# Key softmax of batches 1 to 3 with keys on partitions, short matmul bursts at fixed places, and the second product three pairs behind the first

## The chip, the cores and the metric

The kernel runs on one core of one Trainium2 chip. The metric is the device time in microseconds of one execution. All times here are in us unless marked ns.

## The reference

Four batches of agent attention (12480 queries and keys of 128 channels, 49 agents) feed a two-layer network with an odd nonlinearity.

```python
def attn(q, k, v, agents):                 # B=4, N=12480, C=128, 49 agents
    sm = lambda a, b: softmax((a @ b.transpose(0, 2, 1)) / sqrt(128))
    return sm(q, agents) @ (sm(agents, k) @ v)
def moe(x, w_in, w_out):                   # 49920 tokens, 128 -> 2048 -> 128
    h = x @ w_in
    return (h - tanh(h)) @ w_out
out = moe(attn(q, k, v, agents).reshape(-1, 128), w_in, w_out)
```

All inputs and the output are float32.

## The kernel before

**The main stream.** The 49920 tokens are cut into 100 blocks of 500 (the last block of a batch has 480). The small matrix `agent_v @ w_in` of a batch is formed once (`project`) and split into a rounded part `awh` and a remainder `awl`, so that two fast matmuls (type fp32r) do the work of an exact one. A block then takes 8 *pairs* of 128 hidden channels. One pair is:

- `m1` on TensorE: four matmuls of 500 columns into `h` (PSUM, three buffers), lines 538 and 539;
- `y` (tanh) and `z` (square) on ScalarE, lines 548 and 550; `g = h * z` on VectorE, line 553;
- `gh`, the rounded copy of `g`, on GpSimd, line 582; `gl = g - gh` on VectorE, line 587;
- `m2` on TensorE: six matmuls of 500 columns (lines 600 to 602) that add into the block's accumulator, a `misc` tile in PSUM (two buffers, shared with every short-lived product below).

One pair of every second block (the plain pair) skips the split and uses float32 matmuls at line 598. Two blocks, 16 pairs, make one period of everything else; there are 50 periods.

**Work beside the stream.** In each period, 1000 queries go through a softmax over the agents (`q_softmax`: a burst of 32 small float32 products on TensorE, line 494, which show as 64 matmuls in the trace; then `qm`, `qe`, `qs` and `pp` on VectorE, ScalarE and GpSimd, lines 502 to 517), and are transposed (`q_transpose`, line 525). While batch b runs through the stream, the key softmax of batch b+1 is done in between (`phase1`), in jobs that `fast` starts at three places of a period (`KS` for the scores, `VS` for the rest). A batch has 98 tiles of 128 keys, in 13 groups of 8 tiles (the last of 2).

**The key softmax of batches 1 to 3 before.** The scores of a group lie with *agents* on partitions: `agz` (49 agents padded to 64 columns) is stationary and the keys move past it (line 279); two tiles fill the 128 partitions, 512 columns a group. ScalarE copies them to `s` (281), VectorE takes a maximum (282). After all groups one maximum over everything is formed on VectorE (290 to 295). Then, a group at a time, `av`: ScalarE's exp (324), four transposes on TensorE (330) to bring the keys to partitions, a copy out of PSUM on ScalarE (333), the product with `v` on TensorE (340, whose stationary operand is the transposed e), and an addition into `acc` on VectorE (352).

**Order.** The program is written as generators; each `yield` ends a step, and each pair of the main loop advances every live job by one step. A planner that simulates the engines then sets the order of each engine's queue; `hold` ties an instruction behind another one. Each engine then runs its queue strictly in that order. `LAG1` and `LAG2` say how many pairs `gl` and `m2` are written behind; `NB` gives the numbers of buffers.

Of the kernel before, what the change touches and what calls it, by code (L numbers as in the profile page):

```python
# [12 lines left out]
F32 = mybir.dt.float32  # L13
# [47 lines left out]
LAG2 = 1  # L61
NB = dict(y=2, z=2, g=4, gh=3, gl=2)
# [4 lines left out]
QS = 3  # L67
T0 = 13
T1 = 2
KS = (4, 10, 15)  # L70
VS = (5, 10, 13)
# [26 lines left out]
class Build:  # L98
    def __init__(self, ctx, tc, aps):
# [7 lines left out]
        self.pmisc = ctx.enter_context(self.pool("pmisc", 2, space=PSUM))  # L107

# [9 lines left out]
    def constants(self):  # L118
        nc = self.nc
        c = self.const  # L120
        self.agz = c.tile([128, B, HALF], F32, tag="ag", name="ag")
        self.ag = self.agz[:, :, :A]
        nc.sync.dma_start(self.ag, self.agT.rearrange("b c a -> c b a"))
        nc.gpsimd.memset(self.agz[:, :, A:], 0.0)
# [71 lines left out]
    def phase1(self, b):  # L196
# [36 lines left out]
        def scores(g):  # L233
            yield
            yield
            if g == 0:
                st["s"] = self.keep.tile([128, NG * 512], F32, tag="s", name="s", bufs=1)
                if b == 0:
                    st["mxp"] = self.work.tile([128, A, 2 * NG], F32, tag="mxp", name="mxp", bufs=1)
                else:  # L240
                    st["mxp"] = self.small.tile([128, NG], F32, tag="mxk", name="mxk")
                st["acc"] = self.small.tile([128, C + 1], F32, tag="acc", name="acc")
# [32 lines left out]
            w = n // 2 * 128  # L275
            for c in range(n // 2):
                for r in range(2):
                    to = ps[HALF * r : HALF * (r + 1), c * 128 : (c + 1) * 128]
                    nc.tensor.matmul(to, self.agz[:, b, :], kt[:, n // 2 * r + c, :], start=True, stop=True)  # L279
            yield  # L280
            nc.scalar.copy(st["s"][:, g * 512 : g * 512 + w], ps[:, :w])
            nc.vector.tensor_reduce(st["mxp"][:, g : g + 1], ps[:, :w], axis=AX.X, op=ALU.max)

        def max_in():
            yield
            yield
            if b:
                m = self.small.tile([128, 1], F32, tag="mk", name="mk")
                top = self.small.tile([128, 1], F32, tag="mt", name="mt")
                nc.vector.tensor_reduce(m, st["mxp"], axis=AX.X, op=ALU.max)  # L290
                nc.vector.tensor_copy(top[:HALF], m[HALF:])
                nc.vector.tensor_tensor(m[:HALF], m[:HALF], top[:HALF], ALU.max)
                nc.vector.tensor_copy(m[HALF:], m[:HALF])
                st["mb"] = self.small.tile([128, 1], F32, tag="mn", name="mn")
                nc.vector.tensor_scalar(st["mb"], m, -SCALE, None, ALU.mult)
                return
            m = self.small.tile([128, A], F32, tag="m", name="m")
            nc.vector.tensor_reduce(m, st["mxp"][:, :, 2 * EARLY :], axis=AX.X, op=ALU.max)
# [18 lines left out]
        def av(g):  # L317
            vt = ahead("v", load_v, g, vb - 1) if b else None
            n = tiles(g)
            if b:  # L320
                w = n // 2 * 128
                e = st["s"][:, g * 512 : g * 512 + w]
                first = self.count()
                nc.scalar.activation(e, e, AF.Exp, bias=st["mb"], scale=SCALE)
                self.hold(first, self.act_at, (ET.Activation,))
                yield
                ps = self.misc()
                for c in range(n // 2):
                    sl = slice(c * 128, (c + 1) * 128)
                    nc.tensor.transpose(ps[:, sl], e[:, sl], self.ident)  # L330
                yield
                et = self.small.tile([128, 512], F32, tag="ke", name="ke")
                nc.scalar.copy(et[:, :w], ps[:, :w])
                yield
                ps = self.misc()
                for c in range(n // 2):
                    for r in range(2):
                        t = n // 2 * r + c
                        k = rows(g, t)
                        nc.tensor.matmul(  # L340
                            ps[HALF * r : HALF * (r + 1), : C + 1],
                            et[:k, c * 128 + HALF * r : c * 128 + HALF * (r + 1)],
                            vt[:k, t, : C + 1],
                            start=c == 0,
                            stop=c == n // 2 - 1,
                        )
                yield
                acc = st["acc"]
                if g == 0:
                    nc.vector.tensor_copy(acc, ps[:, : C + 1])  # L350
                else:
                    nc.vector.tensor_tensor(acc, acc, ps[:, : C + 1], ALU.add)
                return
            sv = st["s"][:, g * GT * A : (g * GT + n) * A].rearrange("p (t a) -> p t a", a=A)
            e3 = sv
            nc.vector.tensor_tensor(e3, sv, st["mb"][:, None, :].broadcast_to([128, n, A]), ALU.subtract)
            yield
            nc.scalar.activation(e3, e3, AF.Exp, scale=SCALE)
            yield
# [5 lines left out]
            flat = e3.rearrange("p t a -> p (t a)")  # L365
# [19 lines left out]
            if g in (2, 3):  # L385
                st["es", g % 2] = self.small.tile([128, GT * A], F32, tag="ke", name="es")
# [11 lines left out]
        def sums():  # L398
# [19 lines left out]
            acc = st["acc"]  # L418
# [488 lines left out]
```

## Time and profile before

| | us |
|---|---|
| three runs | 2139.34, 2142.42, 2142.45; median 2142.42 |
| profiled execution | 2142.99, span of the engines' work 2141.2 |
| TensorE matmuls busy | 2107.2 (98%) |
| VectorE busy | 1996.0 (93%) |
| ScalarE busy | 1820.5 (85%) |
| GpSimd busy | 1303.9 (61%) |

The stream's first matmul starts 55.5 us after the span's start; batch 0's key softmax fills the time before it. Matmul ends are modelled, so the busy time of TensorE says only that it is seldom without work; how fast it goes is read from start to start in the timeline. On the other engines a busy time is the engine's own. A wait is put down to the instruction that ended it.

### The profile page before, as it was taken

The page shows a single profiled execution, that of the slowest core. Times are in us where ns is not written, and L with a number is a line of the kernel's source. Part 1 is how long each engine was busy: PE and PEld are TensorE (multiplying, and loading weights), DVE is VectorE, ACT ScalarE, POOL GpSimd, SP SyncE. Part 2 cuts the span into 40 slices and gives each one's busy share as a digit, 9 for nine tenths or more (in the row PEclk, how much of TensorE's full clock was granted, in tenths as well). Part 3 has the DMA queues.
Part 4 walks back from the last instruction along what each step waited for, and adds up shares of the span by engine and source line. Part 5 has one row for each costly group of instructions (what it writes and reads, how often), then busy time and mean ns, then how long its engine had stood idle before and what let it go on. Part 6 is the DMA issues. An engine that isn't in the chain of part 4 may idle for free.

```text
span 2141.2 us, 35133 instructions
## 1 busy us (share of the span) xinstructions
PE 2107.2 (98%) x13259; PEld 1658.2 (77%) x13259; DVE 1996.0 (93%) x2031; ACT 1820.5 (85%) x2136; POOL 1303.9 (61%) x858
## 2 busy tenths in 40 slices
PE   8999999999999999999999999999999999999998
PEld 7577778777777777777787777777777777778776
DVE  7899999889999998889999999988999999999998
ACT  3888888888888888888898888888888989899897
POOL 0366666556665556556576566655666767767666
PEclk9999999999999999999999999999999999999999
DMA  9312112110112111211001110111000000100000
GB/s 343 105 60 68 53 37 72 51 55 24 39 49 67 54 50 50 59 61 49 20 28 61 59 42 30 50 59 42 30 30 21 29 30 20 33 26 20 30 10 21
DMA packets 65345, 109.01 MB, mean 51 GB/s; under 512 B 3984, under 2 KB 44176, under 8 KB 65168
## 3 DMA queue, kind: packets, MB, share of 16 engines
q1 hardware_dynamic: 65168, 106.68, 15.2%
q8 instruction: 108, 1.77, 0.4%
q14 instruction: 69, 0.57, 0.1%
HBM read 81.10 MB, written 25.56 MB: 50 GB/s over the span
## 4 chain that ended last, share of the span: by engine, by line
PE 66%; DVE 18%; issue 6%; POOL 5%; ACT 4%; DMA 0%; POOLq 0%; SPq 0%; DVEq 0%; ACTq 0%
PE misc L602 12%; PE h L538 11%; PE misc L600 11%; PE h L539 11%; PE misc L601 10%; DVE g L553 9%; DVE gl L587 6%; POOL gh L582 4%; PE misc L598 3%; ACT y L548 2%; PE misc L340 2%; PE misc L494 2%; ACT z L550 1%; PE misc L279 1%; PE h L250 1%
## 5 line engine op out<-in xcount | busy, mean ns | idle before, releaser
L582 POOL TENSOR_SCALAR gh<-g 128x1000 fp32r<-128x1000 f32 (+1 forms) x743 | 1197.8, 1612 | 690.2 <-DVE g L553 387.5
L587 DVE TENSOR_TENSOR gl<-g,gh 128x1000 fp32r<-128x1000 f32 (+1 forms) x743 | 956.5, 1287 | 85.6 <-PE misc L602 42.9
L553 DVE TENSOR_TENSOR g<-h,z 128x1000 f32<-128x1000 f32 (+1 forms) x800 | 945.4, 1188 | 30.8 <-ACT z L550 28.8
L548 ACT ACTIVATE y<-h 128x1000 f32<-128x1000 f32 (+1 forms) x800 | 801.4, 1004 | 198.4 <-PE h L539 192.0
L550 ACT ACTIVATE z<-y 128x1000 f32<-128x1000 f32 (+1 forms) x800 | 823.1, 1041 | 29.2 <-DVE g L553 12.9
L538 PE MATMUL h<-pT,awh 98*128 98x500 f32 (+1 forms) x1600 | 662.5, 414 | 0.3
L539 PE MATMUL h<-pT,awl 98*128 98x500 f32 (+1 forms) x1600 | 622.0, 389 | 0.0
L602 PE MATMUL misc<-gl,wo_h 128*128 128x500 f32 (+1 forms) x1486 | 594.4, 400 | 8.2 <-DVE gl L587 7.9
L600 PE MATMUL misc<-gh,wo_l 128*128 128x500 f32 (+1 forms) x1486 | 581.7, 391 | 7.6 <-POOL gh L582 6.7
L601 PE MATMUL misc<-gh,wo_h 128*128 128x500 f32 (+1 forms) x1486 | 578.2, 389 | 0.0
L538 PEld LDWEIGHTS h<-pT,awh 98*128 98x128 f32 x1600 | 301.2, 188 | 79.8 <-issue 17.7
L539 PEld LDWEIGHTS h<-pT,awl 98*128 98x128 f32 x1600 | 303.3, 190 | 68.9 <-issue 14.5
L602 PEld LDWEIGHTS misc<-gl,wo_h 128*128 128x128 f32 x1486 | 279.0, 188 | 83.3 <-DVE gl L587 23.1
L600 PEld LDWEIGHTS misc<-gh,wo_l 128*128 128x128 f32 x1486 | 280.6, 189 | 75.3 <-POOL gh L582 21.6
L601 PEld LDWEIGHTS misc<-gh,wo_h 128*128 128x128 f32 x1486 | 279.7, 188 | 53.6
L505 POOL TENSOR_TENSOR qe<-qe,qm 126x392 f32<-126x392 f32 x50 | 46.9, 938 | 77.2 <-ACT qe L503 77.2
L517 POOL TENSOR_TENSOR pp<-qe,pp 126x392 fp32r<-126x392 f32 x50 | 55.6, 1113 | 59.6 <-ACT pp L515 59.5
L598 PE MATMUL misc<-g,wo_f 128*128 128x500 f32 (+1 forms) x196 | 90.0, 581 | 0.0
L758 ACT ACTIVATE o<-misc 128x500 f32<-128x500 f32 (+1 forms) x100 | 58.0, 580 | 16.2 <-PE misc L602 9.0
L530 ACT CAST pT<-misc 98x500 fp32r<-98x500 f32 (+1 forms) x100 | 56.7, 568 | 5.3 <-PE misc L525 4.4
L598 PEld LDWEIGHTS misc<-g,wo_f 128*128 128x128 f32 x196 | 36.9, 188 | 26.2 <-issue 22.5
L525 PEld LDWEIGHTS misc<-identr,pp 126*98 126x98 f32 x400 | 38.9, 127 | 18.4 <-POOL pp L517 6.5
(111 smaller groups left out, 853.7 us busy)
## 6 DMA issues: line engine op xcount, KB each, us to landing
kt<-kT SPq DMA_DIRECT2D x48, 512.0 KB, 3.7
qt<-qT SPq DMA_DIRECT2D x46, 500.0 KB, 3.5
outT<-o SPq DMA_DIRECT2D x46, 500.0 KB, 2.6
v<-v SPq DMA_DIRECT2D x36, 512.0 KB, 4.1
vt<-v SPq DMA_DIRECT2D x12, 512.0 KB, 5.8
raw<-w_in SPq DMA_DIRECT2D x4, 512.0 KB, 9.2
v<-w_out SPq DMA_DIRECT2D x4, 512.0 KB, 8.1
qt<-qT SPq DMA_DIRECT2D x4, 490.0 KB, 3.5
```

Source lines behind the costliest of these rows:

```text
L538: nc.tensor.matmul(h[:, c, :w], aw[0][:A2, sl], pT[:A2, :w], start=True, stop=False)
L539: nc.tensor.matmul(h[:, c, :w], aw[1][:A2, sl], pT[:A2, :w], start=False, stop=True)
L548: nc.scalar.activation(self.pair(y), h, AF.Tanh, scale=TSC)
L550: nc.scalar.activation(z, y, AF.Square)
L553: nc.vector.tensor_tensor(self.pair(g), h, self.pair(z), ALU.mult)
L582: self.nc.gpsimd.tensor_scalar(gh, g, 1.0, 0.0, ALU.mult, ALU.add)
L587: self.nc.vector.tensor_tensor(gl, g, gh.bitcast(F32), ALU.subtract)
L598: nc.tensor.matmul(acc[:, :w], wf[:, c * C : (c + 1) * C], gh[:, x], start=first, stop=last)
L600: nc.tensor.matmul(acc[:, :w], self.wo_l[:, f, :], gh[:, x], start=first, stop=False)
L601: nc.tensor.matmul(acc[:, :w], self.wo_h[:, f, :], gh[:, x], start=False, stop=False)
L602: nc.tensor.matmul(acc[:, :w], self.wo_h[:, f, :], gl[:, x], start=False, stop=last)
L758: nc.scalar.activation(o[:, at : at + w], acc[n][:, :w], AF.Copy, scale=GSC)
```

## The change

Scores of batches 1 to 3 are now computed with *keys* on partitions: each quarter (32 keys) of a tile of keys is stationary and the 49 agents move, the same shape as the query softmax's burst. A group is 128 partitions by 392 columns in `s`. The maximum is now one for each agent: VectorE reduces each group, and `max_in` and `max_out` (a transpose and a product with a diagonal on TensorE, until now for batch 0 alone) make `mb`. `av` subtracts `mb` on GpSimd, exponentiates on ScalarE three steps later, and two steps after that uses e directly as the stationary operand of the product with `v`; the transposes and the copy behind them are gone.

`burst` chains the small matmuls of the scores, of the product with `v` and of the query scores to one another and behind the last two stream groups written, and `streamed` ties the next six stream groups behind them. `LAG2` goes from 1 to 2, `gh` from 3 to 4 buffers and `gl` from 2 to 3. `QS`, `T1`, `KS` and `VS` are other places; `q_softmax` has one step more ahead of its burst and one less behind it. The tile `s` becomes smaller.

```diff
-LAG2 = 1
-NB = dict(y=2, z=2, g=4, gh=3, gl=2)
+LAG2 = 2
+NB = dict(y=2, z=2, g=4, gh=4, gl=3)
-QS = 3
+QS = 5
-T1 = 2
-KS = (4, 10, 15)
-VS = (5, 10, 13)
+T1 = 3
+KS = (6, 9, 14)
+VS = (2, 5, 9)
...
@@ scores
-            w = n // 2 * 128
-            for c in range(n // 2):
-                for r in range(2):
-                    to = ps[HALF * r : HALF * (r + 1), c * 128 : (c + 1) * 128]
-                    nc.tensor.matmul(to, self.agz[:, b, :], kt[:, n // 2 * r + c, :], start=True, stop=True)
-            yield
-            nc.scalar.copy(st["s"][:, g * 512 : g * 512 + w], ps[:, :w])
-            nc.vector.tensor_reduce(st["mxp"][:, g : g + 1], ps[:, :w], axis=AX.X, op=ALU.max)
+            first = self.count()
+            for t in range(n):
+                for r in range(0, 128, QUART):
+                    to = ps[r : r + QUART, t * A : (t + 1) * A]
+                    nc.tensor.matmul(to, kt[:, t, r : r + QUART], self.ag[:, b, :], start=True, stop=True)
+            self.burst(first)
+            yield
+            nc.scalar.copy(st["s"][:, g * GT * A : (g * GT + n) * A], ps[:, : n * A])
+            nc.vector.tensor_reduce(
+                st["mxp"][:, :, g],
+                ps[:, : n * A].rearrange("p (t a) -> p a t", a=A),
+                axis=AX.X,
+                op=ALU.max,
+            )
...
@@ av
+            first = self.count()
+            (nc.gpsimd if b else nc.vector).tensor_tensor(e3, sv, top, ALU.subtract)
             if b:
-                w = n // 2 * 128
-                e = st["s"][:, g * 512 : g * 512 + w]
-                first = self.count()
-                nc.scalar.activation(e, e, AF.Exp, bias=st["mb"], scale=SCALE)
+                self.hold(first, self.gh_at, (ET.Pool,))
+            yield
+            if b:
+                yield
+                yield
+            first = self.count()
+            nc.scalar.activation(e3, e3, AF.Exp, scale=SCALE)
+            if b:
                 self.hold(first, self.act_at, (ET.Activation,))
                 yield
+            yield
+            if b:
                 ps = self.misc()
-                for c in range(n // 2):
-                    sl = slice(c * 128, (c + 1) * 128)
-                    nc.tensor.transpose(ps[:, sl], e[:, sl], self.ident)
-                yield
-                et = self.small.tile([128, 512], F32, tag="ke", name="ke")
-                nc.scalar.copy(et[:, :w], ps[:, :w])
+                first = self.count()
+                for t in range(n):
+                    r = rows(g, t)
+                    odd = t % 2
+                    w = A if odd else HALF
+                    nc.tensor.matmul(
+                        ps[HALF * odd : HALF * odd + w, : C + 1],
+                        flat[:r, t * A : t * A + w],
+                        vt[:r, t, : C + 1],
+                        start=t < 2,
+                        stop=t >= n - 2,
+                    )
+                self.burst(first)
                 yield
...
+    def burst(self, first):
+        if self.stream is None:
+            return
+        names = [n for group in self.stream[-2:] for n in group]
+        for i in self.queued(first):
+            self.after(i, names)
+            names = [i.name]
+        self.gate = (len(self.stream), names)
+
+    def streamed(self, first):
+        at, names = self.gate
+        group = self.queued(first)
+        if len(self.stream) < at + 6:
+            for i in group:
+                self.after(i, names)
+        self.stream.append([i.name for i in group])
```

On TensorE, at a group of scores of batch 1, the queue of before reads (in a row: line, operation, output and inputs, shape, how many in a row):

```order
L538 MATMUL h<-pT,awh 128x500
L539 MATMUL h<-pT,awl 128x500
L279 MATMUL misc<-kt,ag 64x128 x8
L602 MATMUL misc<-gl,wo_h 128x500
L600 MATMUL misc<-gh,wo_l 128x500
L601 MATMUL misc<-gh,wo_h 128x500
```

With the change, at such a place of the same batch (lines have shifted: 599 to 601 are the stream's second product, 536 and 537 its first):

```order
L601 MATMUL misc<-gl,wo_h 128x500
L278 MATMUL misc<-ag,kt 32x49 x32
L599 MATMUL misc<-gh,wo_l 128x500
L600 MATMUL misc<-gh,wo_h 128x500
L601 MATMUL misc<-gl,wo_h 128x500
```

Eight products of 64 by 128 became 32 of 32 by 49, and they stand inside a run of `m2`.

On GpSimd, in one period of the product with `v` of batch 2, before:

```order
L582 TENSOR_SCALAR gh<-g 128x1000 x11
L505 TENSOR_TENSOR qe<-qe,qm 126x392
L582 TENSOR_SCALAR gh<-g 128x1000 x2
L517 TENSOR_TENSOR pp<-qe,pp 126x8x49
L582 TENSOR_SCALAR gh<-g 128x1000 x13
```

And with the change:

```order
L580 TENSOR_SCALAR gh<-g 128x1000 x9
L321 TENSOR_TENSOR s<-s,mb 128x392
L580 TENSOR_SCALAR gh<-g 128x1000 x3
L321 TENSOR_TENSOR s<-s,mb 128x392
L503 TENSOR_TENSOR qe<-qe,qm 126x392
L580 TENSOR_SCALAR gh<-g 128x1000
L515 TENSOR_TENSOR pp<-qe,pp 126x8x49
```

The subtractions of the keys (line 321) now stand between the `gh`, one of them directly ahead of the queries' `qe`, and one `gh` instead of two stands between `qe` and `pp`.

On ScalarE, in the product with `v` of batch 1, before and then with the change:

```order
L548 ACTIVATE y<-h 128x1000
L333 COPY ke<-misc 128x512
L550 ACTIVATE z<-y 128x1000
L548 ACTIVATE y<-h 128x1000
L550 ACTIVATE z<-y 128x1000
L324 ACTIVATE s<-s,mn 128x512
```

```order
L548 ACTIVATE z<-y 128x1000
L329 ACTIVATE s<-s 128x392
L546 ACTIVATE y<-h 128x1000 x2
L548 ACTIVATE z<-y 128x1000 x2
L501 COPY qe<-misc 126x392
```

The copy `ke` is gone, and the exp works on 392 columns instead of 512.

More of the change, by code (lines that the diff above doesn't have):

```diff
@@ L240, in scores @@
                 else:
-                    st["mxp"] = self.small.tile([128, NG], F32, tag="mxk", name="mxk")
+                    st["mxp"] = st["s"][:, NG * GT * A :][:, : A * NG].rearrange("p (a g) -> p a g", g=NG)
                 st["acc"] = self.small.tile([128, C + 1], F32, tag="acc", name="acc")
@@ L286, in max_in @@
             yield
[L287 to L296, printed above, removed]
             m = self.small.tile([128, A], F32, tag="m", name="m")
-            nc.vector.tensor_reduce(m, st["mxp"][:, :, 2 * EARLY :], axis=AX.X, op=ALU.max)
+            part = st["mxp"] if b else st["mxp"][:, :, 2 * EARLY :]
+            nc.vector.tensor_reduce(m, part, axis=AX.X, op=ALU.max)
             ps = self.misc()
@@ L385, in av @@
             if g in (2, 3):
-                st["es", g % 2] = self.small.tile([128, GT * A], F32, tag="ke", name="es")
+                st["es", g % 2] = self.work.tile([128, GT * A], F32, tag="es", name="es", bufs=2)
             es = st["es", g % 2]
@@ L741, in fast @@
         run(dec[0])
+        self.stream, self.gate = [], (0, [])
         live = []
```

64 lines of the change are left out of this document (31 added, 33 removed).

## The prediction

> **What bounds the kernel now.** I read the page first, then the windows over two quiet stretches, then TensorE's timeline from start to start.
>
> ```profile
> PE 2107.2 (98%) x13259; PEld 1658.2 (77%) x13259; DVE 1996.0 (93%) x2031; ACT 1820.5 (85%) x2136; POOL 1303.9 (61%) x858
> ```
>
> ```profile
> 313.90:444.00 130.10, 130.10 (x873) 103.56 (x872) 114.55 (x118) 113.93 (x135) 77.42 (x52) 1.00 0.19 58
> 1661.00:2051.50 390.50, 388.43 (x2302) 308.60 (x2301) 378.71 (x361) 346.94 (x392) 272.45 (x171) 1.00 0.08 26
> ```
>
> The columns of the windows are length, then busy time of PE, PEld, DVE, ACT and POOL, granted clock, DMA share and GB/s. The first stretch is three periods of batch 1's product with v: PE never without work, DVE at 88%. The second, ten periods of the last batch with no key softmax beside it, has PE at 99.5% and DVE at 97%: there the two are nearly even. A period takes 43.4 in the first (130.10/3) and 39.05 in the second; the key jobs cost what stands between.
>
> ```profile
> 345.49 0.39 PE L601 MATMUL misc<-gh,wo_h 128*128 128x500 f32 x1
> 345.72 0.60 PE L330 MATMUL misc<-ident,s 128*128 128x128 f32 x4
> ...
> 346.60 0.39 PE L538 MATMUL h<-pT,awh 98*128 98x500 f32 x1
> ...
> 1006.12 0.40 PE L601 MATMUL misc<-gh,wo_h 128*128 128x500 f32 x1
> 1006.44 0.90 PE L494 MATMUL misc<-ag,qt 128*32 128x49 f32 x64
> 1007.27 0.50 PE L602 MATMUL misc<-gl,wo_h 128*128 128x500 f32 x1
> ...
> 1007.84 0.39 PE L601 MATMUL misc<-gh,wo_h 128*128 128x500 f32 x1
> ...
> 1203.07 0.40 PE L538 MATMUL h<-pT,awh 98*128 98x500 f32 x1
> ...
> 1205.34 0.40 PE L538 MATMUL h<-pT,awh 98*128 98x500 f32 x1
> ...
> 1221.00 0.39 PE L539 MATMUL h<-pT,awl 98*128 98x500 f32 x1
> 1221.32 1.09 PE L279 MATMUL misc<-kt,ag 128*64 128x128 f32 x16
> 1222.34 0.50 PE L602 MATMUL misc<-gl,wo_h 128*128 128x500 f32 x1
> ...
> 1222.90 0.39 PE L601 MATMUL misc<-gh,wo_h 128*128 128x500 f32 x1
> ```
>
> From one pair's first matmul to the next pair's (1203.07 to 1205.34, ten matmuls) is 2.27, so a large matmul takes 0.227 when nothing waits. What a burst costs the stream is then the time between the large matmuls around it, less their own. Each piece quoted spans three large spacings (0.68) and one burst:
> - old scores, full group: 1222.90 - 1221.00 - 0.68 = 1.22
> - transposes of a full group: 346.60 - 345.49 - 0.68 = 0.43
> - the queries' burst, 64 passes of 32x49: 1007.84 - 1006.12 - 0.68 = 1.04
>
> PE is the engine whose work sets the end, so these are prices on the path.
>
> **The change part by part.**
>
> ```profile
> L494 PE MATMUL misc<-ag,qt 128*32 128x49 f32 (+1 forms) x3200 | 46.1, 210 | 0.0
> L340 PE MATMUL misc<-v,ke 128*64 128x129 f32 (+1 forms) x588 | 42.2, 280 | 0.0
> L279 PE MATMUL misc<-kt,ag 128*64 128x128 f32 x588 | 40.7, 279 | 0.0
> L330 PE MATMUL misc<-ident,s 128*128 128x128 f32 x147 | 22.4, 272 | 0.0
> L311 PE MATMUL misc<-dg,ones 49*128 49x49 f32 x2 | 0.7, 430 | 0.7 <-DVE dg L305 0.7
> L300 PE MATMUL misc<-ident,m 128*49 128x128 f32 x1 | 0.3, 282 | 1.4 <-DVE m L298 1.4
> L505 POOL TENSOR_TENSOR qe<-qe,qm 126x392 f32<-126x392 f32 x50 | 46.9, 938 | 77.2 <-ACT qe L503 77.2
> L281 ACT COPY s<-misc 128x512 f32<-128x512 f32 (+1 forms) x39 | 21.9, 562 | 1.3 <-PE misc L279 1.0
> L324 ACT ACTIVATE s<-s,mn 128x512 f32<-128x512 f32 (+1 forms) x39 | 26.6, 683 | 0.0
> L333 ACT COPY ke<-misc 128x512 f32<-128x512 f32 (+1 forms) x39 | 21.9, 561 | 14.6 <-PE misc L330 14.6
> L507 ACT ACTIVATE qe<-qe 126x392 f32<-126x392 f32 x50 | 26.5, 529 | 0.0
> L503 ACT COPY qe<-misc 126x392 f32<-126x392 f32 x50 | 24.2, 483 | 17.7 <-DVE qm L502 17.7
> L282 DVE TENSOR_REDUCE mxk<-misc 128x1 f32<-128x512 f32 (+1 forms) x39 | 25.3, 649 | 0.0
> L263 DVE TENSOR_REDUCE mxp<-h 128x98 f32<-128x392 f32 (+1 forms) x13 | 6.9, 538 | 1.9 <-ACT s L261 1.9
> ```
>
> 1. Scores. 36 full groups go from 1.22 to the queries' 1.04, since the new burst is 64 passes of the same shape (32 keys stationary, 49 columns moving): 36 x 0.18 = -6.5. Three groups of a quarter of the size: about -0.4, in proportion.
> 2. Transposes. 147 matmuls (36 groups of 4 and 3 of 1) go: 36 x 0.43 + 3 x 0.11 = -15.8.
> 3. Product with v. 588 passes before and after, on two halves of the columns in turn, 129 columns moving: 0. Only the operand's source changes.
> 4. The maximum by agent. Per batch one transpose and one product on PE, both short: rows 300 and 311 give 0.28 + 2 x 0.43 = 1.1 busy, part of which overlaps the stream. Between 0 and 3 x 1.1 I take +2.
>
> PE's work: -6.5 - 0.4 - 15.8 + 2 = -20.7.
>
> 5. Off the path: ACT loses the copy (21.9), and its exp and first copy shrink to the queries' means: 26.6 - 39 x 0.53 = 5.9 and 21.9 - 39 x 0.48 = 3.2, together -31 on an engine at 85%. DVE's reduction falls from 649 to about 538 (row 263, same 392 columns, also strided): -4. Neither ends the period, so 0; if PE stopped being the bound these would still help.
> 6. GpSimd gains 39 subtractions like row 505: 39 x 0.94 = 37 on an engine at 61%; its queue is weighed below. What hides it: in the first window POOL is busy 77.4 of 130.1, and nine subtractions add 8.4.
> 7. The deeper lag and the buffers.
>
> ```profile
> POOL gh L582 <- PE misc L601: 73.3, 100, 3.0
> POOL gh L582 <- PE misc L602: 59.4, 43, 3.6
> DVE gl L587 <- PE misc L602: 42.9, 48, 1.6
> PEld misc L602 <- DVE gl L587: 23.1, 46, 1.2
> PEld misc L600 <- POOL gh L582: 21.6, 35, 1.2
> ```
>
> Columns: who waits for whom, in total, times, longest. PE's real waits in the stream show at the weight loads of m2, the last two rows, 44.7 in all, for `gl` and `gh`. `gl` waits 42.9 for a buffer that m2 still reads, and `gh` up to 132.7 for what may be buffers; a third `gl` and a fourth `gh` take these away. That gives VectorE and GpSimd room to run ahead, but VectorE in the last batch is at 97%: little is left to run ahead with there. Bounds: nothing, or all of 44.7. Nearest rows: the last batch's stretch has PE idle only 2.07 of 390, so most waits lie at the changes from one kind of job to the next, where work on DVE and ACT comes in lumps that a lag of one more pair covers in part. I take -9, a fifth. The waits could also grow, by the rivals' prices below.
> 8. Places of the bursts. The tie adds no instruction. Its cost if a burst's input is late: every `m1` and `m2` behind it on PE waits too, and ScalarE for `h`. Exp is written two pairs (4.5) ahead of its burst and lasts 0.53, so I take 0.
> 9. Batch 0's softmax and SP's loads are the same in number and size: 0.
>
> Sum, against the profiled execution: 2143.0 - 20.7 - 9 = 2113.3. That execution is 0.6 above the median of the runs; against the median, 2112 to 2113. I say 2113.
>
> **The Trainium skill against item 1.** The row first: 64 passes of 49 columns start within 0.83 (1006.44 to 1007.27), 13 ns each. In the Trainium skill, TensorEngine Tiling (Array Packing), section Instruction Overhead, each matmul has about 60 cycles of overhead, and one should not tile a dimension that is already small. TensorE: Matmul & The Clock Gate, section on the clock gate, puts the floor between starts at about 25 ns. By that floor a burst would take 64 x 25 ns = 1.6 instead of 0.83 (an estimate from that page), the scores would cost 36 x 0.59 = 21 more than before, and the sum would be some 28 higher, near 2141. The trace does not agree: four narrow products on separate column strips start side by side.
>
> **The rivals.**
>
> ```profile
> 880.84 0.84 POOL L505 TENSOR_TENSOR qe<-qe,qm 126x392 f32<-126x392 f32 x1 [0.18 <-ACT qe L503]
> 881.26 1.48 DVE L587 TENSOR_TENSOR gl<-g,gh 128x1000 fp32r<-128x1000 f32 x1
> ...
> 888.78 0.96 POOL L517 TENSOR_TENSOR pp<-qe,pp 126x392 fp32r<-126x392 f32 x1 [1.44 <-ACT pp L515]
> ```
>
> ```profile
> 1728.86 1.19 DVE L587 TENSOR_TENSOR gl<-g,gh 128x1000 fp32r<-128x1000 f32 x1
> ...
> 1730.92 0.96 POOL L517 TENSOR_TENSOR pp<-qe,pp 126x392 fp32r<-126x392 f32 x1
> 1731.08 1.86 DVE L587 TENSOR_TENSOR gl<-g,gh 128x1000 fp32r<-128x1000 f32 x1
> ```
>
> A. PE stays the bound and loses 21 of work, waits fall a little: 2113, its own range 2103 to 2123. Chance 0.62.
>
> B. The lag and buffers remove most of the 44.7 of waits: 2143 - 21 - 35 = 2087; with half of them, 2099. For it: 42.9 of buffer waits of `gl`. Against it: DVE at 97% in a quarter of the run. Chance 0.13, for under 2103.
>
> C. VectorE becomes the bound (the other side). A `gl` beside a GpSimd tensor_tensor takes 1.48 (beside `qe`) or 1.86 (beside `pp`) instead of 1.19. So 39 subtractions cost DVE 39 x 0.29 = 11 up to 39 x 0.67 = 26; with their 0.94 ahead of a `gh` in a queue whose `gl` then waits, 37 + 26 = 63. It decides once DVE has no idle left in the product with v: it has 15.5 in 130.1, and nine subtractions take 6 at most while PE's nine sets of transposes give 3.9 back. So it would take about three times the delay seen. If half of it lands: 2143 - 21 + 32 = 2154. Chance 0.07. SBUF — State Buffer, section on its port lock in the Trainium skill, says that DVE with two SBUF inputs and a GpSimd op exclude each other for a whole instruction; the stretch of 0.67 beside 0.96 agrees.
>
> D. Late inputs at the fixed places. In GpSimd's new queue only one `gh` stands between `qe` and `pp`, which lay 8 apart (880.84 to 888.78); a `gh` behind `pp` comes late by up to its own 1.8, and an exp behind a late subtraction holds ScalarE. One pair in that gap is the plain one, without `gh`, which speaks against it. In 12 such periods 12 x 1.8 = 22 would eat the gain of the waits and more: 2143 - 21 + 22 = 2144 at worst, and half of it gives 2133. Chance 0.15, mostly at 2123 to 2138.
>
> E. The narrow passes do not start side by side. A pass of the old burst takes 64 ns (1221.32 to 1222.34, 16 passes), one of the queries' 13 ns; at twice the latter a group would take 1.66 instead of 0.83, 36 x 0.83 = 30 more, and the sum would be 2143. The queries' row has the very shape, so 0.03.
>
> **How the numbers follow.** A's value is the forecast. The range, 2093 to 2137, leaves out the lower half of B (0.06), C, E and the upper end of D (0.04): 0.2 in all. Under 0.2% (4.3 of 2142.4) this kernel's measurement can't tell a change from none. Faster than 2138.1: A, B and 0.11 of D, 0.86. Within 0.2%: 0.03 of D, and E, 0.06. Slower: C and the last 0.01 of D, 0.08.
>
> **What would show it.** In the profile after: transposes gone from PE and the scores at about 1.04 a group between large matmuls; periods of the product with v near 42.1 instead of 43.4 (less 3 x 0.43) and of the scores about 0.5 shorter; the last batch's periods between 38.3 and 39; PE waits for `gl` and `gh` below 44.7; DVE below 97% beside the key softmax. Wrong, if `gl`'s mean rises past 1.5, if PE waits for line 329's exp, or if the last batch's period grows.

## The result, and the profile after

The change makes the kernel slower: 2154.11 (median; 2153.68 to 2156.22) against 2141.84 before, a ratio of 1.0061 [1.0049, 1.0074]. The profiled execution's span is 2152.4, 11.2 more than before. The forecast was 2113.

First the engines on the page, then the windows of the changed kernel: the product with v of batch 1, three periods of scores of batch 3, and ten periods of the last batch.

```profile
PE 2089.7 (97%) x14885; PEld 1635.8 (76%) x14885; DVE 1989.5 (92%) x2028; ACT 1795.2 (83%) x2097; POOL 1378.3 (64%) x896
```

```profile
309.20:443.50 134.30, 129.12 (x840) 101.45 (x839) 119.12 (x119) 109.14 (x128) 87.76 (x61) 0.99 0.18 56
1170.10:1301.70 131.60, 129.50 (x1268) 97.17 (x1267) 119.63 (x118) 107.87 (x127) 74.43 (x52) 1.00 0.17 54
1680.60:2064.20 383.60, 383.60 (x2302) 309.19 (x2301) 377.17 (x362) 347.90 (x391) 284.12 (x171) 1.00 0.08 26
```

And the same three periods of scores in the kernel before:

```profile
1156.60:1281.80 125.20, 125.00 (x830) 98.77 (x829) 118.78 (x117) 107.33 (x126) 75.86 (x51) 1.00 0.18 56
```

The last batch's period fell from 39.05 to 38.36. But a period of scores grew from 41.7 to 43.9, and one of the product with v from 43.4 to 44.8, although TensorE has less to do in both. VectorE's busy time in the scores is the same (118.8 and 119.6), in 6.4 more of time: it stands idle more.

To split the gain from the loss I take the length of each period from its first `m1` to the next one's, and subtract TensorE's work at steady prices (0.227 for a large matmul, each burst whole and at what it costs the stream where nothing waits). What is left is waiting:

| waits of TensorE's stream | scores (14 periods) | product with v, batches 1, 2 (10) | batch 3 (5) | change of batch (8) | last batch (12) | all 50 periods | work |
|---|---|---|---|---|---|---|---|
| before | 11.8 | 6.0 | 4.0 | 9.1 | 11.5 | 47.6 | 2031.8 |
| after | 25.9 | 21.8 | 2.0 | 22.5 | 3.1 | 80.8 | 2011.1 |

The work fell by 20.7. The waits rose by 33.2: 14.1 in the scores, 15.8 in the product with v, 13.4 at the changes of batch, less 8.4 in the last batch and 2.0 in batch 3 (and 0.2 more in the first period, which the table leaves out). The stream starts 1.4 earlier. -20.7 + 33.2 - 1.4 = 11.1, the difference of the spans.

Where the waits are, from the list of waits of after (who waits for whom, total, times, longest), and then two of its counterparts before. PEld is TensorE's loading of the stationary operand; its waits do not all lengthen the run: for line 341 they are 21.8 at the loads and 15.9 at the matmuls.

```profile
DVE gl L586 <- POOL gh L580: 91.4, 122, 1.9
ACT qe L501 <- DVE qm L500: 74.2, 30, 5.4
PEld misc L601 <- DVE gl L586: 23.4, 43, 2.0
PEld misc L341 <- ACT qe L501: 21.8, 14, 2.4
PEld misc L599 <- POOL gh L580: 21.3, 54, 1.0
PE misc L341 <- ACT qe L501: 15.9, 14, 2.0
PE h L536 <- DVE g L551: 7.8, 12, 1.3
PE misc L492 <- issue: 4.4, 1, 4.4
```

```profile
DVE gl L587 <- POOL gh L582: 37.6, 43, 1.2
ACT qe L503 <- DVE qm L502: 17.7, 21, 4.2
```

**The product with v.** Line 341 waits 14 times for the *queries'* copy (line 501), which has nothing to do with its inputs. The timeline of one such place, batch 2:

```profile
930.12 0.90 PE L492 MATMUL misc<-ag,qt 128*32 128x49 f32 x64
...
932.11 1.20 DVE L586 TENSOR_TENSOR gl<-g,gh 128x1000 fp32r<-128x1000 f32 x1 [0.93 <-POOL gh L580]
...
933.23 1.19 DVE L551 TENSOR_TENSOR g<-h,z 128x1000 f32<-128x1000 f32 x1
934.34 0.56 DVE L500 TENSOR_REDUCE qm<-misc 126x8 f32<-126x392 f32 x1
...
934.93 0.49 ACT L501 COPY qe<-misc 126x392 f32<-126x392 f32 x1 [2.81 <-DVE qm L500]
...
935.47 1.09 PE L341 MATMUL misc<-v,s 128*64 128x129 f32 x16 [1.99 <-ACT qe L501]
```

The queries' burst fills a `misc` buffer at 930.12. Two engines must read it before it is free: VectorE's `qm`, behind two `gl` and a `g` in its queue, and then ScalarE's copy, which starts when `qm` has ended. There are two `misc` buffers, and the other one is the block's accumulator. With `VS = (2, 5, 9)` a product with v, which comes five pairs behind the start of its job, stands one pair behind the queries' burst. It gets its output buffer at 935.4, after TensorE has waited 1.99, and everything tied behind it on TensorE is late with it.

**The change to the projection of batch 3** has the same mechanism, with a longer holder:

```profile
1566.50 0.39 PE L418 MATMUL misc<-sel,acc 113*128 113x49 f32 x2
...
1567.98 0.20 DVE L421 TENSOR_SCALAR sm<-misc 128x49 f32<-128x49 f32 x1
...
1572.84 0.26 DVE L424 TENSOR_TENSOR avs<-misc,sm 128x98 f32<-128x98 f32 x1
...
1573.20 1.53 PE L492 MATMUL misc<-ag,qt 128*32 128x49 f32 x64 [4.42 <-issue]
```

The short products of `sums` take the buffer at 1566.50, VectorE reads it a last time at 1572.84, and the queries' burst right behind waits 4.42. The list names no releaser for this wait; that it is the buffer is read from the times here, and tested by moving `sums` (e13 below).

The other changes of batch were not taken apart by a run. There `m1` itself, and not only its load, waits for VectorE's `g`, a row that the list of before does not have: 5.0 of the 7.8 lie in four periods at a change of batch.

**The clock.** Beside this wait, and behind one of the 14 of line 341, the granted clock falls to half for one window of 3.4:

```profile
418.80:422.60 3.80, 3.80 (x18) 2.99 (x13) 3.80 (x5) 2.21 (x4) 3.20 (x3) 0.55 0.47 134
1572.84:1576.26 3.42, 3.06 (x68) 2.71 (x69) 0.82 (x3) 0.49 (x1) 1.27 (x2) 0.51 0.18 31
```

Each costs up to another 1.7, half of the window. Between 60 and 2130 the kernel before has none.

### The profile page after: what moved, and what is told of

It is laid out like the page before. It is cut to its first block, busy times and chain, and to the rows that moved or that the text cites. A ratio compares the mean times of both kernels' runs of the same rounds, so it can differ in the third digit from the quotient of the medians.

```text
span 2152.4 us, 38228 instructions
## 1 busy us (share of the span) xinstructions
PE 2089.7 (97%) x14885; PEld 1635.8 (76%) x14885; DVE 1989.5 (92%) x2028; ACT 1795.2 (83%) x2097; POOL 1378.3 (64%) x896
## 4 chain that ended last, share of the span: by engine, by line
PE 70%; DVE 15%; POOL 6%; issue 6%; ACT 3%; DMA 0%; POOLq 0%; DVEq 0%; SPq 0%; ACTq 0%
PE h L536 13%; PE h L537 12%; PE misc L599 12%; PE misc L601 12%; PE misc L600 11%; DVE g L551 8%; POOL gh L580 5%; DVE gl L586 4%; PE misc L597 3%; PE misc L341 2%; ACT z L548 1%; PE misc L492 1%; ACT y L546 1%; PE misc L523 1%; PE h L249 1%
## 5 line engine op out<-in xcount | busy, mean ns | idle before, releaser
L580 POOL TENSOR_SCALAR gh<-g 128x1000 fp32r<-128x1000 f32 (+1 forms) x743 | 1218.6, 1640 | 611.2 <-DVE g L551 499.9
L586 DVE TENSOR_TENSOR gl<-g,gh 128x1000 fp32r<-128x1000 f32 (+1 forms) x743 | 937.2, 1262 | 100.4 <-POOL gh L580 91.4
L536 PE MATMUL h<-pT,awh 98*128 98x500 f32 (+1 forms) x1600 | 654.5, 409 | 7.9 <-DVE g L551 7.8
L599 PE MATMUL misc<-gh,wo_l 128*128 128x500 f32 (+1 forms) x1486 | 594.6, 400 | 5.9 <-ACT o L783 3.0
L601 PE MATMUL misc<-gl,wo_h 128*128 128x500 f32 (+1 forms) x1486 | 584.9, 394 | 7.7 <-DVE gl L586 7.6
L599 PEld LDWEIGHTS misc<-gh,wo_l 128*128 128x128 f32 x1486 | 280.5, 189 | 83.6 <-POOL gh L580 21.3
L601 PEld LDWEIGHTS misc<-gl,wo_h 128*128 128x128 f32 x1486 | 279.7, 188 | 78.4 <-DVE gl L586 23.4
L503 POOL TENSOR_TENSOR qe<-qe,qm 126x392 f32<-126x392 f32 x50 | 65.5, 1309 | 61.4 <-ACT qe L501 61.4
L597 PE MATMUL misc<-g,wo_f 128*128 128x500 f32 (+1 forms) x196 | 91.4, 588 | 0.0
L501 ACT COPY qe<-misc 126x392 f32<-126x392 f32 x50 | 24.1, 482 | 74.2 <-DVE qm L500 74.2
L492 PEld LDWEIGHTS misc<-ag,qt 128*32 128x32 f32 (+1 forms) x3200 | 39.3, 112 | 24.9 <-issue 17.6
```

The costliest lines, as they stand in the source:

```text
L503: nc.gpsimd.tensor_tensor(ev, ev, m[:TT, :, None].broadcast_to([TT, GT, A]), ALU.subtract)
L536: nc.tensor.matmul(h[:, c, :w], aw[0][:A2, sl], pT[:A2, :w], start=True, stop=False)
L580: self.nc.gpsimd.tensor_scalar(gh, g, 1.0, 0.0, ALU.mult, ALU.add)
L586: self.nc.vector.tensor_tensor(gl, g, gh.bitcast(F32), ALU.subtract)
L597: nc.tensor.matmul(acc[:, :w], wf[:, c * C : (c + 1) * C], gh[:, x], start=first, stop=last)
L599: nc.tensor.matmul(acc[:, :w], self.wo_l[:, f, :], gh[:, x], start=first, stop=False)
```

## The experiments

Each is timed against the kernel before on the same chip (2140.4 to 2141.7). All diffs are against the changed kernel, unless said.

### The place of the product with v

`e4_other_vs`

```diff
-VS = (2, 5, 9)
+VS = (4, 7, 11)
```

> The changed kernel with VS = (4, 7, 11) instead of (2, 5, 9), so that the bursts of the product with v stand at pairs 9, 12 and 0 of a period and none right behind the queries' burst at pair 6; all else stays. P: the waits of line 341 go, 44.4 to 44.7 a period in batches 1 and 2 becomes about 42.3, nine periods, -20 us, and with the slow clock 2130 to 2134. G: scores stay at 43.9 and gl's wait at about 91 us in either case, and if G alone holds no change, 2150 to 2156. K: no change.

Measured: 2132.96, ratio 0.996 [0.9946, 0.9974], 21 less than the change. Three periods of batch 1's product with v:

```profile
311.80:438.50 126.70, 126.70 (x840) 100.50 (x839) 119.04 (x119) 109.77 (x128) 91.87 (x61) 1.00 0.19 59
```

The mean period is 42.2 and the last two are 41.95, close to the 42.1 that the forecast had for TensorE's work alone. Line 341's waits for line 501 are gone, and so is the half-speed window behind them; the waits of batches 1 and 2 fall from 21.8 to 3.4. The scores are as before the edit (25.1 of waits). So the place cost 21 on balance, and the scores are another matter.

`e5_qm_from_copy` leaves the place and shortens the hold: ScalarE's copy goes first, and VectorE reduces the copy instead of the PSUM buffer.

```diff
-        nc.vector.tensor_reduce(m[:TT], pv, axis=AX.X, op=ALU.max)
         nc.scalar.copy(ev, pv)
+        nc.vector.tensor_reduce(m[:TT], ev, axis=AX.X, op=ALU.max)
```

> The changed kernel with the queries' maximum qm taken from the copy in SBUF instead of PSUM, so that the queries' misc buffer is freed by ScalarE's copy alone, which no longer waits for VectorE; places and ties stay. P: ScalarE's wait for qm (74 us, up to 5.4 each) and the waits of line 341 (16 us) go, 2154 - 25 = about 2129. G and K: qm only moves one step later, 2150 to 2158.

Measured: 2149.17, 1.0034 [1.002, 1.0048]. The waits of line 341 for the queries' copy are gone here too, but another takes most of their place:

```profile
PEld misc L601 <- DVE gl L586: 36.9, 67, 2.0
```

The loads of `m2` now wait more for `gl` (23.4 before the edit). In batch 1 the first two periods of the product with v fall from 43.7 and 44.7 to 41.9 and 43.0, but the last two still take 45.2; those of the scores fall to 41.7. Taking away the named wait is not the same as taking away the lateness: VectorE's queue was late as well. Both edits together, `e6_vs_and_qm`:

> The changed kernel with VS = (4, 7, 11) and the queries' maximum qm taken from the copy in SBUF. The first alone gave 2133 (product-with-v periods 41.95, scores still 43.9), the second alone gave scores at 41.7 but 45.2 in the product with v. If the two losses are separate (Theory P for the product with v, and for the scores VectorE standing idle for gh in front of gl, which the other place of qm in the queues mends), both periods are short: 2133 - 9 periods x 2.1 = about 2114. If they are one thing that only moves from place to place, 2125 to 2140.

Measured: 2123.93, 0.9922 [0.9909, 0.9936]: scores 41.7, product with v about 42.9. That lies just under the 2125 to 2140 of a loss that only moves, and well above the 2114 of two separate ones.

### The buffers

`e7_vs_old_buffers`, `e11_vs_gh4` and `e12_vs_gl3` all have `VS = (4, 7, 11)`, and with e4 they make the four combinations of `gh` and `gl`.

```diff
-NB = dict(y=2, z=2, g=4, gh=4, gl=3)
+NB = dict(y=2, z=2, g=4, gh=3, gl=2)   # e7; e11: gh=4, gl=2; e12: gh=3, gl=3
```

> The changed kernel with VS = (4, 7, 11) and the old numbers of buffers (gh 3, gl 2), LAG2 = 2 kept. If the third gl buffer lets VectorE's queue put two gl in a row ahead of g and wait for gh (Theory G, buffers), the scores go from 43.9 to about 41.6 a period, 9 periods, 2133 - 20 = 2113, less what the last batch loses (up to 13 x 0.7 = 9). If buffers are a help only, the waits for a free buffer come back: 2133 to 2150.

> Products with v at pairs 4, 7, 11; gh four buffers, gl back to two. Theory (the third gl buffer lets VectorE's order put two gl in a row ahead of g, and the queue then stands before an unready gh): scores stretches fall from 43.9 to about 42.1 per two blocks and the time is near 2121. Rival (the fourth gh buffer is what shifts GpSimd's order): scores stay at 43.9, 2132 to 2135.

> Products with v at pairs 4, 7, 11; gl three buffers, gh back to three. Theory of the third gl buffer: scores stay near 43.9 per two blocks, time 2132 to 2135, gl waits for gh near 80 us in all. Rival of the fourth gh buffer: scores 42.1, time near 2121.

| | gl = 2 | gl = 3 |
|---|---|---|
| gh = 3 | 2119.84 (0.9903 [0.9888, 0.9919]) | 2134.26 (0.9967 [0.9955, 0.9978]) |
| gh = 4 | 2119.38 (0.9899 [0.9882, 0.9916]) | 2132.96 (0.996 [0.9946, 0.9974]) |

The third `gl` costs 14, the fourth `gh` nothing. Three periods of scores, in e11 and then in e12:

```profile
1138.70:1264.90 126.20, 124.29 (x1268) 99.23 (x1267) 119.48 (x118) 107.65 (x127) 78.32 (x52) 1.00 0.18 56
```

```profile
1147.80:1279.60 131.80, 129.42 (x1268) 97.08 (x1267) 119.56 (x118) 107.94 (x127) 74.35 (x52) 1.00 0.17 54
```

VectorE's work is equal, and only its idle time differs. In these stretches `gl` waits for `gh` 6 times with two buffers (4.1 in all) and 16 times with three (10.7); with three, `m2` on TensorE waits 5.1 for `gl`, with two not visibly. In the changed kernel's timeline GpSimd and VectorE work there in lumps:

```profile
1213.32 1.20 DVE L586 TENSOR_TENSOR gl<-g,gh 128x1000 fp32r<-128x1000 f32 x1
1215.44 1.20 DVE L586 TENSOR_TENSOR gl<-g,gh 128x1000 fp32r<-128x1000 f32 x1 [0.92 <-POOL gh L580]
1216.56 2.30 DVE L551 TENSOR_TENSOR g<-h,z 128x1000 f32<-128x1000 f32 x2
```

```profile
1217.91 3.16 POOL L580 TENSOR_SCALAR gh<-g 128x1000 fp32r<-128x1000 f32 x2 [2.50 <-DVE g L551]
```

Two `gl` stand in a row, and the second waits for its `gh`; the `g` behind them come late, so GpSimd has nothing for 2.5 and then has two to do. This is only part of it. With two buffers the queue has such pairs too (6 in e11's stretch, 8 in e12's). Of e12's 16 waits six stand directly behind another `gl` (5.6 in all) and ten elsewhere, nearly all behind a short job (5.1); of e11's six it is three and three (2.8 and 1.4). So the third buffer changes the order of VectorE's queue and the new order waits more: that is shown. Why the planner then chooses the worse order is not.

### The lag

`e1_old_lag` (the old lag and buffers at the new places), `e8_vs_old_lag` (the old lag at the other places) and `e9_before_lag2` (the kernel before with the longer lag alone):

```diff
-LAG2 = 2
+LAG2 = 1            # e1 and e8; e9: before with LAG2 = 2
-NB = dict(y=2, z=2, g=4, gh=4, gl=3)
+NB = dict(y=2, z=2, g=4, gh=3, gl=2)   # e1 alone
-VS = (2, 5, 9)
+VS = (4, 7, 11)     # e8 alone
```

> The changed kernel with LAG2 = 1 and the old numbers of gh and gl buffers (3 and 2); the keys on partitions, the ties and the places stay. Theory P (a burst of the product with v is tied close behind the queries' burst and waits for the misc buffer that the queries' copy frees late): the waits of line 341 for that copy stay near 16 us on PE, and the last batch's periods go back from 38.3 to about 39.0, so 2154 + 9 = about 2163. Theory G (the deeper lag lets VectorE's queue put gl ahead of a gh that is not ready): gl's wait for gh falls from 91 to about 38 us, the scores' periods fall from 43.9 to about 41.5, so about 2154 - 20 + 9 = 2143. Theory K (the subtraction on GpSimd slows VectorE): no large change, 2150 to 2163.

> The changed kernel with VS = (4, 7, 11), LAG2 = 1 and the new numbers of buffers. With LAG2 = 1 and the old places, 2226 was measured, the last batch at 40.4 a period. If the ties need the deeper lag (m2 tied in front of or behind a burst has no slack at two pairs), about 2180 to 2215 here, the last batch still 40.4. If the old places of VS or the old buffers made that loss, 2133 to 2150.

> The kernel before with LAG2 = 2 alone (no ties, agents on partitions, old places and buffers). If the deeper lag is itself good, as forecast, the last batch goes from 39.05 to about 38.3 a period and the waits at the changes of jobs shrink: 2142 - 9 = 2133. If the lag alone does nothing, since the planner had already put m2 three and two thirds pairs behind, 2140 to 2145. If it harms VectorE's order (Theory G), 2150 to 2165.

Measured: e1 2225.59, 1.0394 [1.0376, 1.0411]; e8 2173.15, 1.0153 [1.0137, 1.0168]; e9 2138.43, 0.9989 [0.998, 0.9998]. e1 lies far above what any of its three theories gave, e8 a little under its 2180 to 2215, e9 between 2133 and 2140. Alone the lag is worth 0.1%. With the fixed places it is worth 40 (e8 against e4): without it the last batch's period is 40.4. The waits of TensorE's weight loads in e1, and of line 341:

```profile
PEld misc L601 <- DVE gl L586: 61.1, 104, 2.0
PEld misc L599 <- POOL gh L580: 49.4, 91, 1.0
PE misc L341 <- ACT qe L501: 27.6, 14, 2.1
```

Behind each burst six groups of the stream are fixed, and with one pair less of distance their `gl` and `gh` are late more often. e1 is 52 above e8: at its places line 341's waits for the queries' copy are longer than in the changed kernel (15.9), and nine of them, with one of line 492, go with a half-speed window; e8 has no wait of line 341 for that copy.

### The fixed places and the keys

`e3_no_ties` is the change without `burst` and `streamed`; `e14_best_no_ties` is e7 without them; `e10_keys_alone` is only the keys on partitions with e stationary: no ties, and lag, buffers, starts and the queries' steps as before.

```diff
-        self.stream, self.gate = [], (0, [])
+        self.gate = (0, [])        # stream stays None: no ties
```

> The changed kernel without the ties of the bursts to the stream (the planner places them freely); places, lag and buffers stay. P: the planner moves the late burst behind m2 work, the waits of line 341 for the queries' copy go, about 25 us (14 waits of 1.75 and the slow clock after one of them), 2129. G and K: no gain from this, 2150 to 2158.

> Only the keys on partitions with e stationary: no fixed places, the second product two pairs behind, three gh and two gl buffers, the queries' steps and the starts of key groups and of products with v as before. Theory (the softmax part is sound; what the change loses is lost by the fixed places of the bursts and by the two added buffers): the scores and transposes give back the 22 us of PE work that the profile after shows, product-with-v stretches near 42 per two blocks, last batch at the old 39.0 to 39.6: 2118 to 2128. Rival (the GpSimd subtractions of the key softmax delay gh and so VectorE in every block of batches 1 to 3): gl waits for gh above 80 us in all and a time of 2140 or more.

> Products with v at pairs 4, 7, 11, three gh and two gl buffers, lag two, but no fixed places: the 64 passes of a group may be split by products of the blocks, as in the run with the keys alone. Theory (the places keep the bursts whole, and whole bursts are what the scores' saving and the smooth last batch rest on): last batch 39.3 to 39.7 per two blocks instead of 38.3 (some 13 us), scores above 42.5, time 2135 to 2145. Rival (the places are worth nothing beside the longer lag): 2118 to 2124, as with them.

Measured: e3 2148.96, 1.0038 [1.0024, 1.0053]; e10 2148.93, 1.0035 [1.0021, 1.005]; e14 2171.2, 1.0141 [1.0124, 1.0157].

In e3 most periods of the product with v take 42.0 at the very places of the change: line 341, free to stand later in the queue, nowhere waits for line 501. What it loses is in the scores of batch 3 (43.9) and the last batch (39.6).

e10 fits neither theory. The saving in TensorE's work by the steady prices, each burst taken whole, is there (2011.1), and yet it is 7 slower than before. The rival's sign is absent (`gl` waits 41.3 for `gh`, not 80). The timeline shows one group of its scores, whose 64 passes go in four pieces with large matmuls between:

```profile
1202.98 0.46 PE L278 MATMUL misc<-ag,kt 128*32 128x49 f32 x22
...
1204.93 0.38 PE L278 MATMUL misc<-ag,kt 128*32 128x49 f32 x16
...
1206.78 0.46 PE L278 MATMUL misc<-ag,kt 128*32 128x49 f32 x22
...
1208.29 0.28 PE L278 MATMUL misc<-ag,kt 128*32 128x49 f32 x4
```

The groups by shape tell the sum of it, in e10 and then in the changed kernel:

```profile
L278 PE MATMUL misc<-ag,kt 128*32 128x49 f32 x2352 | 47.4, 211 | 0.0
```

```profile
L278 PE MATMUL misc<-ag,kt 128*32 128x49 f32 x2352 | 33.6, 209 | 0.0
```

The 39 groups go in 96 pieces. They cost the stream 49.4 in all, against 39.2 whole, about 0.18 for each further piece. The products with v are split as well (55 pieces, 49.2 against 42.7 whole in e7). That is 17 of the 27 by which e10's waits exceed those of before; where the other 10 come from is open.

e14 shows the price of splitting in the good version: 51 more than e7, where 15 to 25 were expected. The queries' bursts go in 130 pieces instead of 50, and the ten periods of the last batch take 401.6 instead of 383.7, in e7 and then in e14:

```profile
1644.90:2028.60 383.70, 383.70 (x2302) 308.95 (x2301) 377.67 (x362) 347.79 (x391) 283.73 (x171) 1.00 0.08 26
1676.70:2078.30 401.60, 396.64 (x2302) 308.57 (x2301) 390.82 (x361) 349.74 (x391) 275.70 (x171) 1.00 0.07 25
```

VectorE's busy time grows by 13 there with the same instructions, and `gl` alone accounts for it (1.32 at the mean against 1.23 in e7; 30 of its 150 take over 1.3, against 10). Of these 30, 20 run beside a GpSimd `tensor_tensor`, as all 10 in e7 do. So the splits may not be all of the loss; that the free order lays more of VectorE's work beside GpSimd's fits the trace, and no run tests it. How the 51 divide was not settled, nor why e3, with more buffers and other places, loses less.

### What is left in the good version

`e13_sums_later` is e7 with `sums` one step later in batch 3; `e15_places_by_batch` is e7 with the old places of the product with v in batch 3.

```diff
-        jobs += [av(g) for g in range(NG)] + [None] * (b > 0) + [sums()]
+        jobs += [av(g) for g in range(NG)] + [None] * ((b > 0) + (b == 3)) + [sums()]   # e13
-            if pos in (VS if len(kq) < nv else KS) and kq and 0 < n:
+            if pos in ((2, 5, 9) if b == 2 and len(kq) < nv else VS if len(kq) < nv else KS) and kq and 0 < n:   # e15
```

> The version with products with v at pairs 4, 7, 11 and three gh and two gl buffers, and in batch 3 the product sums one place later, so that it no longer stands right ahead of the queries' burst. Theory (a burst on the heels of another waits until the two-engine release of its buffer): the wait of 4.4 us at the change to the projection goes, and the clock window behind it: 2114 to 2117. Rival (the wait only moves to the next burst or to the chain behind sums): 2119 to 2121, as without it.

> As the version at pairs 4, 7, 11 with three gh and two gl buffers, but batch 3 with its products with v at pairs 2, 5, 9. Theory (in batch 3, where the order of the blocks is shifted, the old places are the ones clear of other work: 42.3 per two blocks there with them, 44.25 without): four stretches gain 1.9 each, 2112 to 2115. Rival (the 44.25 come from the fewer buffers, not from the places): 2119 to 2121.

e13: 2117.26, 0.9888 [0.9872, 0.9905], not separable from e7. The queries' burst in e7 and then in e13, with the clock over the place in e13:

```profile
1540.34 1.53 PE L492 MATMUL misc<-ag,qt 128*32 128x49 f32 x64 [3.31 <-issue]
```

```profile
1538.43 0.90 PE L492 MATMUL misc<-ag,qt 128*32 128x49 f32 x64
```

```profile
1520.00:1610.00 90.00, 88.55 (x499) 67.53 (x498) 85.33 (x90) 77.26 (x89) 59.34 (x37) 1.00 0.07 24
```

The wait and the half-speed window are gone and the period falls from 45.6 to 40.2, but the next period rises from 40.9 to 44.7: of 5.4, 3.8 return as waits spread over `m2`. Here the rival was nearly right.

e15: 2115.41, 0.9876 [0.986, 0.9893], the fastest measured, 0.2% under e7, though the two intervals still touch. Batch 3's three periods in e7 and then in e15:

```profile
1345.30:1477.10 131.80, 129.69 (x836) 97.78 (x835) 120.35 (x117) 106.55 (x126) 88.67 (x61) 1.00 0.17 53
```

```profile
1346.40:1472.20 125.80, 125.80 (x836) 99.83 (x835) 116.47 (x118) 108.46 (x127) 93.02 (x61) 1.00 0.17 52
```

43.9 a period against 41.9, so batch 3's slower periods in e7 come from the places; at the change of batch 4.0 of the gain is lost again. The buffers have a part in it: with three `gl` the same three periods take 129.5 at the places 4, 7, 11 (e4) and 127.0 at 2, 5, 9 (the changed kernel). So the other places cost 6.0 in batch 3 with two `gl`, and 2.6 with three.

The places of the scores (`KS`), of the queries' burst (`QS` and its added step) and of the transposes (`T1`) were not changed one by one, so what each of them adds is open.

## Why the prediction was wrong

**Steps 1 to 4, TensorE's work: right.** The forecast was -20.7, and the traces give 2011.1 - 2031.8 = -20.7 with every burst whole. (The 0.4 for the three small groups was too much: a quarter of 0.18 for each is 0.14 in all.) A full group of scores costs what the queries' did:

```profile
1215.47 0.39 PE L601 MATMUL misc<-gl,wo_h 128*128 128x500 f32 x1
1215.80 0.90 PE L278 MATMUL misc<-ag,kt 128*32 128x49 f32 x64
...
1217.18 0.39 PE L601 MATMUL misc<-gl,wo_h 128*128 128x500 f32 x1
```

1217.18 - 1215.47 - 0.68 = 1.03. The fixed places earn this: step 1 counted whole bursts as given, and e10 shows that without ties they are not.

**Step 6, and rivals C and E: right to hold them small.** The subtractions took 1.08 at the mean instead of 0.94 (1.14 for the 36 full ones), and `gl`'s mean fell; its row before stands last:

```profile
L321 POOL TENSOR_TENSOR s<-s,mb 128x392 f32<-128x392 f32 (+1 forms) x39 | 42.3, 1083 | 0.0
L586 DVE TENSOR_TENSOR gl<-g,gh 128x1000 fp32r<-128x1000 f32 (+1 forms) x743 | 937.2, 1262 | 100.4 <-POOL gh L580 91.4
L587 DVE TENSOR_TENSOR gl<-g,gh 128x1000 fp32r<-128x1000 f32 (+1 forms) x743 | 956.5, 1287 | 85.6 <-PE misc L602 42.9 <-POOL gh L582 37.6 <-POOL qe L505 1.5
```

That C's figure, 2154, is the measured time is luck: what it rests on, a slower `gl`, did not come. On GpSimd the queries' own subtraction grew as well, from 0.94 to 1.31, which step 6 did not have; no run shows what that cost.

**Step 8, the places: this step failed.** It asked only whether a burst's *input* is late, priced the exp, and took 0. The exp was in time: TensorE waited 0.5 in all for line 329, and that in batch 0, ahead of the stream. What came late was the burst's *output buffer*, still held by the burst ahead of it. With the clock it cost 21 in the products with v (e4), and about 5 at batch 3's change (5.4 in its period, by e13 against e7), of which e13 could keep little. Rival D was the nearest (fixed places delay the stream, 2133 to 2144), but by the input, and its price was too small. At the same time step 8 missed the gain of the places: without them the good version is 51 slower (e14). A term set to 0 was the largest of all, in both signs.

**Step 7, lag and buffers: this step failed in its sign.** It took -9, at the changes from one kind of job to the next; the stream's waits grew by 33.2, of them 13.4 at the changes of batch. "Nothing, or all of 44.7" were both on the side of gain; the step said that the waits could grow, and gave that no price of its own. The 44.7, the loads' waits for `gl` and `gh`, is the same after (23.4 + 21.3). The waits for a buffer that `m2` still reads did go, as argued (42.9 for `gl` to none), but they had not been what cost time: e7 has the old buffers and is faster. What the third `gl` did was to change VectorE's order; `gl`'s waits for `gh` grew from 37.6 to 91.4 (with two buffers, in e7, 59.6), and it cost 14, most of it in the scores.

In the last batch the waits fell by 8.4, and that this is near the -9 is luck: the step expected little there, and the gain is not the buffers', since e7 has the same period with the old ones. The lag alone brings the period from 39.05 to 38.9 (e9), the lag without the fixed places leaves 39.6 (e3), the fixed places without the lag 40.4 (e8); both together give 38.36. The lag's own share was misread too: alone it is worth 2 in all (e9), and it is needed to bear the ties.

None of the three signs named as "wrong, if" came: `gl` stayed under 1.5, TensorE hardly waited for the exp, and the last batch's period fell. The signs were drawn from the mechanisms already thought of. It was the signs for a right forecast that failed: the shorter periods beside the key softmax, and loads' waits below 44.7. With other places and two `gl` buffers, e7 and e15 come to 2119.84 and 2115.41, near the 2113 forecast for the change: the two edits of e7 give back 34 of the 41 by which the forecast was short.

## What to carry to other kernels

A burst that is fixed to a place needs its output buffer as well as its input: ask who held that buffer last, which engines must read it in turn, and what stands ahead of them in their queues. A second short burst one step behind another, with one free buffer between them, waits for the whole release. One more buffer is not a free gain where a planner sets the order: the order changes with it, and here the new one cost 14. Count small matmuls by pieces and not by passes: the same 2352 passes cost the stream 39.2 whole and 49.4 in pieces.

## What the hardware showed

The granted clock fell to half for one window of 3.41 behind a stretch of 4.4 without a matmul (up to 1573.20), and once behind a wait of only 1.98 (418.17), while the 13 other waits of line 341, up to 2.0 long, were followed by none. In e1 it fell so ten times inside the stream, each time with a wait of only 1.6 to 2.05. In the Trainium skill, TensorE: Matmul & The Clock Gate, Part 1 on the clock gate, the half rate comes after an idle window of about 3.4, and the window runs free of the program. The length of the window agrees with the trace, and so does the wait of 4.4; the case at 1.98 and the ten of e1 are shorter than the rule's idle window. That the windows run free of the program agrees too: the two half-speed windows of the changed kernel start at 419.09 and 1572.80, 338 times 3.413 apart. On this grid the wait from 416.19 to 418.17 lies whole inside the window ahead of 419.09, while the three others as long (they end at 464.15, 935.47 and 979.83) are cut by the edge of a window. So here a wait of 2 was enough where it fell into one window.

VectorE's `qm` and ScalarE's copy both only read the same PSUM buffer, and the copy began when the reduction had ended (934.34 + 0.56, then 934.93). PSUM — Partial Sum Buffer in the Trainium skill, section PSUM bank collisions raise a hardware error, says that the compiler's scheduler adds a dependency between two engines' accesses to one bank and quadrant, reads as well; the trace agrees, 30 waits of `qe` for `qm` with 74.2 in all. So here a release by two readers takes the sum of their times, not the longer one.
